# Two decode layers: evacuations on ACT alone, another order of the last weight tiles, and a parked weight copied back by one engine

## The chip, the cores and the metric

One core of a Trainium2 chip runs the whole program. Time is device microseconds of one execution; lower is better. All data is fp32. PE is the matmul engine, DVE and ACT are the two engines that can read the matmul's accumulators in PSUM, SP issues the DMAs.

## The reference

Batch 8, one new token each, two layers that share their weights. A layer is attention over a cache of 4096 keys (32 query heads, 4 key heads, 128 wide) and then a GELU network of 3584 hidden columns, each with a layernorm ahead and a residual.

```python
x = A_x                                   # [8, 1, 1024]
x = x + _A_ref(_layernorm(x), k_cache, v_cache, wq, wo)   # q = x@wq, softmax(q k) v, @wo
x = x + _B_ref(_layernorm(x), w1, b1, w2, b2)             # gelu(x@w1 + b1) @ w2 + b2
x = x + _A_ref(_layernorm(x), k_cache, v_cache, wq, wo)
x = x + _B_ref(_layernorm(x), w1, b1, w2, b2)
```

## The kernel before

All that is read from memory goes through one list of transfers (`stream`), written out by hand with a fixed place for each in one large SBUF tile, `arena` (52 units of 128 x 1024). `pump` issues the transfers in that order on SP's queue: the next one goes out as soon as its place is free, and what is behind it in the list waits. A place becomes free where the program calls `release`, behind the last matmul that reads it. So PE's order decides when SP may issue.

Since only 8 rows of x are there, matmuls use 32 of the array's columns, and four of them work side by side on four column groups, which write the four 32-row quarters of one PSUM bank. An fp32 matmul stands in the trace as two rows.

- `expand` (L256): h = x @ w1 in seven groups `u` of 512 hidden columns. A group's eight matmuls (L263) read one w1 tile of 2 MB; the accumulator is scaled into a row, half by DVE (L273) and half by ACT (L274); `hidden_group` transposes it (L284), sums its quarters (L330), and computes bias and GELU on DVE and ACT up to h (L336), eight columns of `hT` for each of 28 tiles `kt`. `work` is a table of what stands between the matmuls of a group and behind its evacuation. In layer 1 the last w1 tile comes in two halves.
- `down` and `down_row`: h @ w2. w2 lies in four blocks `c` of 256 output columns. Most of it is read once, in layer 0, and stays for layer 1; the first four tiles of each block (kind `"u"`, 512 KB each) are read again for layer 1 and are the last four transfers of the program. `down_row` (L389) multiplies tiles of h with all four blocks, block `c` in column group `c`. `grow_u` does this for the pieces, one block after the other.
- `swap` is between the layers. It finishes the w2 blocks of layer 0 one by one (L383), copies each (L426), turns it with PE (L430) and adds it to x (L432); as soon as two tiles `kt` of x are there, it multiplies them with wq for layer 1 (`used`, L299), tile by tile and for two accumulators `u`, and so frees the places in which wq lay since the start. `late` holds one such step until behind the next block's copy. The places are taken by w2's own blocks 1 to 3 and, behind them, by the first tiles of k of layer 1.
- The last wq tile doesn't fit in the arena: `park` keeps a part of it in PSUM (`spot`, 128 x 2048) and a part in the SBUF tile `spare`. `unpark` (L647, L648) copies `spot` back to the arena, into the place of wq tile (3,1).

Of the kernel before, what the change touches and what calls it, by code (L numbers as in the profile page):

```python
# [9 lines left out]
AF = mybir.ActivationFunctionType  # L10
ALU = mybir.AluOpType
# [4 lines left out]
B, D = 8, 1024  # L16
# [4 lines left out]
NFT = F // P  # L21
CH = 512
HALF = SK // 2
NH = SK // HALF
W = HALF // P * DH
# [16 lines left out]
CB = D // Q4  # L42
# [3 lines left out]
NGR = F // G  # L46
GT = G // P
# [57 lines left out]
def decode_layers(ctx: ExitStack, tc: tile.TileContext, x, kc, vc, wq, wo, w1, w2, out):  # L105


    nc = tc.nc
# [38 lines left out]
    hT = oT  # L147
# [107 lines left out]
    def expand(name, rs, lag, work={}):  # L255
        rows = [row_s, qz[:, 2 * GT * B:2 * GT * B + CH]]  # L256
        for u in range(NGR):
            acc = ps_o.tile([P, CH], F32, tag="o", name="acc")
            kt = 0
            for i, slot in enumerate(tiles((name, u))):  # L260
                for c in range(0, slot.cols, G):
                    j = kt % 4
                    nc.tensor.matmul(acc[32 * j:32 * j + 32, :], xnT[:, kt * XS:kt * XS + 32], slot.ap[:, c:c + G],  # L263
                                     start=(kt < 4), stop=(kt >= NT - 4))
                    kt += 1
                release(slot)
                for f in work.get((u, i), ()):
                    f()
            assert kt == NT
            row = rows[u % 2]  # L270
            if u == 0:
                flush()
            nc.vector.tensor_scalar(row[:, 0:CH // 2], acc[:, 0:CH // 2], rs, None, op0=ALU.mult)  # L273
            nc.scalar.activation(row[:, CH // 2:], acc[:, CH // 2:], AF.Copy, scale=rs)  # L274
            if lag:
                flush()
            pending.append(lambda u=u, row=row: hidden_group(u, row))
            for f in work.get(u, ()):
                f()
# [25 lines left out]
    def queries(rs):  # L305
# [16 lines left out]
            into_qz(u, lambda e, dst: nc.vector.tensor_copy(dst, src[:, e * REP:(e + 1) * REP, 0:B]))  # L322
        rows.free()

    def hidden_group(u, row):
        src = turned(row).rearrange("p (t j) q -> p t q j", j=4)[:, :, 0:B]
        t0 = u * GT
        pre, g = qz[:, 0:GT * B], qz[:, GT * B:2 * GT * B]
        pre_v = pre.rearrange("p (t b) -> p t b", b=B)
        nc.vector.tensor_reduce(pre_v, src, AX.X, ALU.add)  # L330
        nc.vector.tensor_tensor(pre_v, pre_v, b1T[:, t0:t0 + GT].unsqueeze(2).to_broadcast([P, GT, B]), ALU.add)
        nc.vector.tensor_tensor(g, pre, pre, ALU.mult)
        nc.vector.scalar_tensor_tensor(g, g, 1.0 / GELU_A, pre, op0=ALU.add, op1=ALU.mult)
        nc.scalar.activation(g, g, AF.Tanh, scale=GELU_C * GELU_A)
        nc.vector.tensor_scalar(pre, pre, 0.5, None, op0=ALU.mult)
        nc.vector.scalar_tensor_tensor(hT[:, t0 * B:(t0 + GT) * B], g, 1.0, pre, op0=ALU.add, op1=ALU.mult)  # L336
        if u == NGR - 1 and st["layer"] == 0:
            nc.gpsimd.memset(qz[:, 0:2 * GT * B + CH], 0.0)

# [37 lines left out]
    w2_at = {}  # L377

    def down(y, c, kts, n0=0):

        for n, kt in enumerate(kts, n0):
            g = kt % 4
            nc.tensor.matmul(y[32 * g:32 * g + 32], hT[:, kt * B:kt * B + 32], w2_at[c, kt], start=(n < 4), stop=(n >= NFT - 4))  # L383

    def down_row(y, kts, cs=range(CB)):

        for kt in kts:
            for c in cs:
                nc.tensor.matmul(y[32 * c:32 * c + 32], hT[:, kt * B:kt * B + 32], w2_at[c, kt],  # L389
                                 start=st["y0"][c], stop=(kt == NFT - 1))  # L390
                st["y0"][c] = False

    def arrive(c, kind):
        kts = W2_KTS[kind]
# [5 lines left out]
    def swap():  # L400

        ys = small_ps("s")
        down(ys[:, 0:Q4], 0, arrive(0, "u"), 0)
        flush()
        nc.vector.tensor_tensor(xv, xv, b2T.unsqueeze(2).to_broadcast([P, NT, B]), ALU.add)
        pt = small_ps("pt")
        late = []
        acc = q_acc()
        stats = ()

        def used(kt, u):
            slot = held.pop(("q", kt, u))
            q_part(acc, u, kt, 0, slot.ap)
            release(slot)
            if (kt, u) == (3, 1):
                st["unparked"] = unpark()

        for c in range(CB):
            y = ys[:, c % 2 * Q4:(c % 2 + 1) * Q4]
            kts = []  # L420
            for kind in W2_ORDER[c]:
                kts += arrive(c, kind) if c or kind != "u" else []
            down(y, c, kts, NFT - len(kts))
            release(held.pop(("w2u0", c)))
            ysb = row_s[:, c % 2 * Q4:(c % 2 + 1) * Q4]
            nc.vector.tensor_copy(ysb, y)  # L426
            while late:
                late.pop()()
            for i in range(2):
                nc.tensor.matmul(pt[:, i * B:(i + 1) * B], ysb[:, i * P:(i + 1) * P], bsel, start=True, stop=True)  # L430
            xc = xv[:, 2 * c:2 * c + 2]
            nc.vector.tensor_tensor(xc, pt[:, 0:2 * B].rearrange("p (i b) -> p i b", b=B), xc, ALU.add)  # L432
            if c == CB - 1:
                stats = moments(pt)
            for kt in (2 * c, 2 * c + 1):
                for u in range(2):
                    if kt < NT - 1:
                        late.append(lambda kt=kt, u=u: used(kt, u))
                        if c == CB - 1 or (kt, u) not in ((1, 1), (3, 1)):
                            late.pop()()  # L440
                    elif u == 0:
                        spot = st.pop("unparked")
                        q_part(acc, u, kt, 0, spot.ap)
                        spot.free()
                    else:
                        slot = held.pop(("qe", 0))
                        q_part(acc, u, kt, 0, slot.ap[:, 0:W - KEEP])
                        q_part(acc, u, kt, W - KEEP, spare)
                        slot.free()
                    if c == CB - 1 and (kt, u) in ((NT - 2, 1), (NT - 1, 0)):  # L450
                        next(stats, None)
        arena.own_at = OWN[1]
        dl, rs, tmp = (oT[:, a:a + n] for a, n in ((192, B), (200, B), (0, REP * B)))
        rows = arena.own()
        row = [rows.ap[:, u * CH:(u + 1) * CH] for u in range(2)]
        nc.vector.tensor_copy(row[0], acc[0])
        nc.scalar.activation(row[1], acc[1], AF.Copy)
        for u in range(2):
            src = turned(row[u], ("s", "pt")[u])

            def emit(e, dst):
                t = src[:, e * REP:(e + 1) * REP]
                v = tmp.rearrange("p (t b) -> p t b", b=B)
                nc.vector.tensor_tensor(v, t[:, :, B:XS].to_broadcast([P, REP, B]), dl.unsqueeze(1).to_broadcast([P, REP, B]), ALU.mult)
                nc.vector.tensor_tensor(v, t[:, :, 0:B], v, ALU.subtract)
                nc.vector.tensor_tensor(dst, v, rs.unsqueeze(1).to_broadcast([P, REP, B]), ALU.mult)

            into_qz(u, emit)
        rows.free()
# [174 lines left out]
    def unpark():  # L644
        spot = st.pop("spot")
        slot = arena.take(2, OWN[1][0:1])
        nc.scalar.activation(slot.ap[:, 0:W // 2], spot[:, 0:W // 2], AF.Copy)  # L647
        nc.vector.tensor_copy(slot.ap[:, W // 2:], spot[:, W // 2:])  # L648
        return slot

    def weights(name, dram, sizes, starts, c0=0, i0=0, kept=None):
# [85 lines left out]
    for layer in range(2):  # L737
# [9 lines left out]
        if layer == 0:  # L747
            expand("i0", rs, True)
            swap()
        else:  # L750
            nc.vector.tensor_tensor(x_row, x_row, b2_row, ALU.add)
            y = []

            def grow(u):
                if not y:
                    y.append(small_ps("s")[:, 0:Q4])
                    st["y0"] = [True] * CB
                down_row(y[0], groups[u])

            def grow_u(*cs):  # L760
                for c in cs:
                    arrive(c, "u")
                    down_row(y[0], groups[0], [c])

            groups = [range(GT * u, GT * (u + 1)) for u in range(NGR)]
            work = {0: [flush], 1: [flush], **{u: [lambda u=u: grow(u - 1), flush] for u in range(2, NGR - 1)},
                    (NGR - 1, 0): [lambda: grow(NGR - 2)], NGR - 1: [flush, lambda: grow_u(*range(CB))]}
            expand("i1", rs, False, work)
            down_row(y[0], groups[NGR - 1])
            nc.vector.tensor_tensor(x_row, x_row, y[0], ALU.add)  # L770

    nc.sync.dma_start(out=out, in_=x_row)
# [68 lines left out]
```

## Time and profile before

| | |
|---|---|
| median of 3 runs | 859.35 us (859.25 to 860.32) |
| the profiled execution | 858.83 us, its span 856.9 us |
| PE, DVE, ACT busy | 539.4, 198.8, 63.4 us |
| DMA | 359.55 MB, mean 420 GB/s |
| granted PE clock, mean | 0.801 |

The span is the stretch from the first to the last instruction on the profiled core; the execution's own time is 1.9 us longer. Times in rows of the trace are counted from the span's start. A row of the timeline has start, duration, engine, line, operation, out<-in, shape and count, and in brackets how long the engine had been idle and who ended that. Rows that follow each other and overlap are merged with their count.

### The profile page before, as it was taken

Reading aid. Unit: us, or ns where it says so; the run is one execution under the profiler, and the core shown is the slowest. Engines: PE = TensorE matmul, PEld = TensorE weight load, DVE = VectorE, ACT = ScalarE, POOL = GpSimd, SP = SyncE. Lnnn points to the kernel's source line nnn. Section 1 sums busy time; section 2 is a strip of 40 time slices with the busy share of each in tenths; the row PEclk is TensorE's granted clock in tenths of the full one; section 3 lists DMA queues with packets and bytes.
Section 4 is the critical chain, followed back from the end, with each engine's and each line's share of the span. In section 5 each row is a group of like instructions: output and inputs, shape, how many; then the busy total and the mean of one; then the engine's idle time right before and its main releaser. Section 6 shows DMA issues by size and latency. Waiting matters only on the chain.

```text
span 856.9 us, 9313 instructions
## 1 busy us (share of the span) xinstructions
PE 539.4 (63%) x4002; PEld 185.5 (22%) x4002; DVE 198.8 (23%) x689; ACT 63.4 (7%) x136; POOL 2.2 (0%) x13
## 2 busy tenths in 40 slices
PE   0766665576665656755778786556565484664687
PEld 0212121121212111222233233112111121121333
DVE  0012232222222122300320342223212132231032
ACT  0110000000000000001101100000000000000020
POOL 0000000000000000000000000000000000000000
PEclk9976877867876768788888987769778687787889
DMA  9999999999999999999999999999999999999994
GB/s 398 420 437 435 419 436 428 426 431 427 428 429 433 434 431 426 424 428 426 423 397 360 423 434 423 450 418 431 432 426 426 431 428 448 420 425 433 421 424 194
DMA packets 19768, 359.55 MB, mean 420 GB/s; under 512 B 2192, under 2 KB 2576, under 8 KB 3600
## 3 DMA queue, kind: packets, MB, share of 16 engines
q1 hardware_dynamic: 19584, 358.82, 98.4%
q8 instruction: 31, 0.51, 0.2%
q10 hardware_dynamic: 144, 0.15, 0.1%
q14 instruction: 9, 0.07, 0.0%
HBM read 358.83 MB, written 0.13 MB: 419 GB/s over the span
## 4 chain that ended last, share of the span: by engine, by line
DMA 72%; PE 23%; DVE 2%; issue 1%; ACT 1%; another core or an unknown queue 1%; SPq 0%; ACTq 0%; DVEq 0%
DMA arena<-in_k_dram 27%; DMA arena<-in_v_dram 22%; DMA arena<-in_wo_dram 10%; DMA arena<-in_w_dram 9%; PE sps L509 8%; PE o_ps L565 7%; DMA arena<-in_wq_dram 5%; PE acc L299 2%; PE y L346 2%; PE sps L389 1%; PE sps L541 1%; PE acc L263 1%; PE sps L383 1%; ACT arena L532 1%
## 5 line engine op out<-in xcount | busy, mean ns | idle before, releaser
L565 PE MATMUL o_ps<-arena 128*32 128x512 f32 x1024 | 165.8, 772 | 83.0 <-DMA arena<-in_v_dram 82.9
L509 PE MATMUL sps<-arena,qz 128*32 128x512 f32 x1024 | 149.3, 724 | 95.2 <-DMA arena<-in_k_dram 93.8
L509 PEld LDWEIGHTS sps<-arena,qz 128*32 128x32 f32 x1024 | 32.7, 125 | 177.2 <-DMA arena<-in_k_dram 100.5
L570 DVE SCALAR_TENSOR_TENSOR scr<-o_ps,bits,scr 128x128 f32<-128x128 f32 x192 | 67.4, 351 | 6.8
L565 PEld LDWEIGHTS o_ps<-arena 128*32 128x32 f32 x1024 | 33.7, 131 | 147.9 <-issue 115.1
L568 DVE TENSOR_SCALAR scr<-o_ps,bits 128x128 f32<-128x128 f32 x64 | 22.5, 351 | 171.4 <-PE o_ps L565 171.4
L532 ACT ACTIVATE arena<-arena,bits 128x512 f32<-128x512 f32 x32 | 22.8, 714 | 525.0 <-DVE scr L527 525.0
L346 PE MATMUL y<-arena,oxT 128*32 128x256 f32 x512 | 40.7, 478 | 32.6 <-DMA arena<-in_wo_dram 32.6
L514 DVE TENSOR_SCALAR_CACHE_REDUCE arena<-sps 128x512 f32<-128x512 f32 x32 | 22.1, 692 | 147.8 <-PE sps L509 147.8
L541 PE MATMUL sps<-ident,arena 128*128 128x128 f32 x128 | 28.9, 382 | 24.6 <-ACT arena L532 24.3
L263 PE MATMUL acc<-arena,oxT 128*32 128x512 f32 x224 | 34.6, 743 | 14.2 <-DMA arena<-in_w_dram 13.7
L299 PE MATMUL acc<-arena,oxT 128*32 128x512 f32 (+1 forms) x250 | 35.7, 707 | 6.6 <-DMA arena<-in_wq_dram 3.5
L577 PEld LDWEIGHTS sps<-bits,scr 128*128 128x128 f32 x128 | 20.7, 203 | 66.6 <-issue 36.9
L346 PEld LDWEIGHTS y<-arena,oxT 128*32 128x32 f32 x512 | 18.6, 133 | 52.4 <-DMA arena<-in_wo_dram 36.1
L578 DVE TENSOR_TENSOR oxT<-sps,scr 128x8 f32<-128x8 f32 x64 | 10.6, 165 | 72.5 <-PE sps L577 72.5
L541 PEld LDWEIGHTS sps<-ident,arena 128*128 128x128 f32 x128 | 20.3, 190 | 30.3 <-ACT arena L532 30.2
L577 PE MATMUL sps<-bits,scr 128*128 128x8 f32 x128 | 26.5, 280 | 0.0
L523 PE MATMUL sps<-scr,bits 128*128 128x128 f32 x32 | 8.3, 344 | 22.8 <-DVE scr L519 22.8
L545 DVE COPY arena<-sps 128x512 f32<-128x512 f32 x16 | 11.1, 692 | 29.7 <-PE sps L541 29.7
L383 PE MATMUL sps<-arena,oxT 128*32 128x256 f32 x224 | 14.8, 398 | 4.4 <-DMA arena<-in_w_dram 4.4
L199 PE MATMUL sps<-ident,xb 128*128 128x128 f32 x6 | 1.5, 345 | 24.6 <-DMA xb<-in_x_dram 23.5
L389 PE MATMUL sps<-arena,oxT 128*32 128x256 f32 x224 | 15.9, 380 | 0.6 <-DVE oxT L336 0.6
(115 smaller groups left out, 221.0 us busy)
## 6 DMA issues: line engine op xcount, KB each, us to landing
arena<-in_v_dram SPq DMA_DIRECT2D x19, 4096.0 KB, 18.6
arena<-in_k_dram SPq DMA_DIRECT2D x31, 2048.0 KB, 17.3
arena<-in_k_dram SPq DMA_DIRECT2D x12, 4096.0 KB, 17.5
arena<-in_w_dram SPq DMA_DIRECT2D x17, 2048.0 KB, 12.6
arena<-in_v_dram SPq DMA_DIRECT2D x4, 6144.0 KB, 25.4
arena<-in_v_dram SPq DMA_DIRECT2D x11, 2048.0 KB, 20.6
arena<-in_wo_dram SPq DMA_DIRECT2D x10, 2048.0 KB, 12.6
arena<-in_k_dram SPq DMA_DIRECT2D x2, 6144.0 KB, 23.6
```

What stands on the lines that cost most here:

```text
L263: nc.tensor.matmul(acc[32 * j:32 * j + 32, :], xnT[:, kt * XS:kt * XS + 32], slot.ap[:, c:c + G], start=(kt < 4), stop=(kt >= NT - 4))
L299: nc.tensor.matmul(acc[u][32 * j:32 * j + 32, d0 - j * CH:d1 - j * CH], xnT[:, kt * XS:kt * XS + 32], ap[:, d0 - c0:d1 - c0], start=(kt == ...
L346: nc.tensor.matmul(y[32 * j:32 * j + 32, 0:Q4], lhs[:, n * B:n * B + 32], slot.ap[:, c + j * Q4:c + (j + 1) * Q4], start=(n == 0), stop=(n ...
L383: nc.tensor.matmul(y[32 * g:32 * g + 32], hT[:, kt * B:kt * B + 32], w2_at[c, kt], start=(n < 4), stop=(n >= NFT - 4))
L389: nc.tensor.matmul(y[32 * c:32 * c + 32], hT[:, kt * B:kt * B + 32], w2_at[c, kt], start=st["y0"][c], stop=(kt == NFT - 1))
L509: nc.tensor.matmul(ps[32 * g:32 * g + 32, :], qz[:, c:c + 32], kt[:, g * CH:(g + 1) * CH], start=(j == 0), stop=(j == HKV - 1))
L532: nc.scalar.activation(part, part, AF.Exp, bias=bias, scale=1.0, accum_out=ls[:, h:h + 1])
L541: nc.tensor.transpose(pp[:, t * P:(t + 1) * P], row[:, c:c + P], ident)
L565: nc.tensor.matmul(o[32 * g:32 * g + 32, :], s[:, g], v[:, g * CH:(g + 1) * CH], start=(half == 0), stop=(half == NH - 1))
L568: nc.vector.tensor_scalar(r, o[:, 0:P], sel_t[:, 0:1], None, op0=ALU.mult)
L570: nc.vector.scalar_tensor_tensor(r, o[:, t * P:(t + 1) * P], sel_t[:, t:t + 1], r, op0=ALU.mult, op1=ALU.add)
L577: nc.tensor.matmul(po[:, 0:REP], r_s[j % 2], sel_h, start=True, stop=True)
```

## The change

- In `expand` ACT alone scales all 512 columns of a group into the row; DVE's half is gone (14 instructions on DVE in both layers, and the one in `unpark`).
- In layer 1's end both halves of the last w1 tile are multiplied at once. The w2 products of group 5 follow in two halves, one ahead of and one behind the transposes of the last group; then those of group 6; and the four late pieces (group 0) at the very end, tile by tile over the four blocks.
- h of the last group goes to columns of `spare` in layer 1.
- In `swap`, wq (1,1) is no longer held back, `spot` is copied back by ACT alone, and that step is called behind wq (4,0) in place of (3,1).

```diff
-            nc.vector.tensor_scalar(row[:, 0:CH // 2], acc[:, 0:CH // 2], rs, None, op0=ALU.mult)
-            nc.scalar.activation(row[:, CH // 2:], acc[:, CH // 2:], AF.Copy, scale=rs)
+            nc.scalar.activation(row, acc, AF.Copy, scale=rs)
...
+    def h_at(kt):
+        if st["layer"] and kt >= NFT - GT:
+            return spare[:, 2 * CH + (kt - NFT + GT) * B:]
+        return hT[:, kt * B:]
...
-    def down_row(y, kts, cs=range(CB)):
+    def down_row(y, kts):
         for kt in kts:
-            for c in cs:
-                nc.tensor.matmul(y[32 * c:32 * c + 32], hT[:, kt * B:kt * B + 32], w2_at[c, kt],
-                                 start=st["y0"][c], stop=(kt == NFT - 1))
-                st["y0"][c] = False
+            for c in range(CB):
+                nc.tensor.matmul(y[32 * c:32 * c + 32], h_at(kt)[:, 0:32], w2_at[c, kt],
+                                 start=(kt == GT), stop=(kt == GT - 1))
...
-            if (kt, u) == (3, 1):
+            if (kt, u) == (4, 0):
                 st["unparked"] = unpark()
...
-                        if c == CB - 1 or (kt, u) not in ((1, 1), (3, 1)):
+                        if (kt, u) != (3, 1):
                             late.pop()()
...
-        nc.scalar.activation(slot.ap[:, 0:W // 2], spot[:, 0:W // 2], AF.Copy)
-        nc.vector.tensor_copy(slot.ap[:, W // 2:], spot[:, W // 2:])
+        nc.scalar.activation(slot.ap, spot, AF.Copy)
...
-            def grow_u(*cs):
-                for c in cs:
-                    arrive(c, "u")
-                    down_row(y[0], groups[0], [c])
+            end = groups[NGR - 2]
             work = {0: [flush], 1: [flush], **{u: [lambda u=u: grow(u - 1), flush] for u in range(2, NGR - 1)},
-                    (NGR - 1, 0): [lambda: grow(NGR - 2)], NGR - 1: [flush, lambda: grow_u(*range(CB))]}
+                    NGR - 1: [lambda: down_row(y[0], end[:2]), flush, lambda: down_row(y[0], end[2:])]}
             expand("i1", rs, False, work)
             down_row(y[0], groups[NGR - 1])
+            for c in range(CB):
+                arrive(c, "u")
+            down_row(y[0], groups[0])
```

PE's order in `swap`, from the first block's w2 to the third block's turn, before (x12 at L299 are three wq steps of four matmuls, x28 at L383 a block of w2, x2 at L430 the turn):

```order
L383 MATMUL sps<-arena,oxT 32x256 x24
L430 MATMUL sps<-bits,scr 128x8 x2
L299 MATMUL acc<-arena,oxT 32x512 x12
L383 MATMUL sps<-arena,oxT 32x256 x28
L299 MATMUL acc<-arena,oxT 32x512 x4
L430 MATMUL sps<-bits,scr 128x8 x2
L299 MATMUL acc<-arena,oxT 32x512 x12
```

The same place after:

```order
L388 MATMUL sps<-arena,oxT 32x256 x24
L434 MATMUL sps<-bits,scr 128x8 x2
L298 MATMUL acc<-arena,oxT 32x512 x16
L388 MATMUL sps<-arena,oxT 32x256 x28
L434 MATMUL sps<-bits,scr 128x8 x2
L298 MATMUL acc<-arena,oxT 32x512 x12
```

wq (1,1), four matmuls, has moved from behind block 1's w2 to ahead of it.

PE's order at the end of the program, before (L263 is w1, L284 the transposes, L389 w2; scr and qz are the two rows that take turns):

```order
L284 MATMUL sps<-ident,qz 128x128 x4
L263 MATMUL acc<-arena,oxT 32x512 x4
L389 MATMUL sps<-arena,oxT 32x256 x16
L263 MATMUL acc<-arena,oxT 32x512 x4
L284 MATMUL sps<-ident,scr 128x128 x4
L389 MATMUL sps<-arena,oxT 32x256 x32
```

The same place after:

```order
L283 MATMUL sps<-ident,qz 128x128 x4
L263 MATMUL acc<-arena,oxT 32x512 x8
L394 MATMUL sps<-arena,oxT 32x256 x8
L283 MATMUL sps<-ident,scr 128x128 x4
L394 MATMUL sps<-arena,oxT 32x256 x8
L394 MATMUL sps<-arena,spare 32x256 x16
L394 MATMUL sps<-arena,oxT 32x256 x16
```

The last four matmuls with w1 stand directly behind the first four; group 5's sixteen with w2 are split around the transposes; the late pieces are the last sixteen, where before they were the first sixteen of the last 32. SP's order of transfers is the same in both.

More of the change, by code (lines that the diff above doesn't have):

```diff
@@ L335, in hidden_group @@
         nc.vector.tensor_scalar(pre, pre, 0.5, None, op0=ALU.mult)
-        nc.vector.scalar_tensor_tensor(hT[:, t0 * B:(t0 + GT) * B], g, 1.0, pre, op0=ALU.add, op1=ALU.mult)
+        nc.vector.scalar_tensor_tensor(h_at(t0)[:, 0:GT * B], g, 1.0, pre, op0=ALU.add, op1=ALU.mult)
         if u == NGR - 1 and st["layer"] == 0:
@@ L382, in down @@
             g = kt % 4
-            nc.tensor.matmul(y[32 * g:32 * g + 32], hT[:, kt * B:kt * B + 32], w2_at[c, kt], start=(n < 4), stop=(n >= NFT - 4))
-    def down_row(y, kts, cs=range(CB)):
+            nc.tensor.matmul(y[32 * g:32 * g + 32], h_at(kt)[:, 0:32], w2_at[c, kt], start=(n < 4), stop=(n >= NFT - 4))
+    def down_row(y, kts):
         for kt in kts:
-            for c in cs:
-                nc.tensor.matmul(y[32 * c:32 * c + 32], hT[:, kt * B:kt * B + 32], w2_at[c, kt],
-                                 start=st["y0"][c], stop=(kt == NFT - 1))
-                st["y0"][c] = False
+            for c in range(CB):
+                nc.tensor.matmul(y[32 * c:32 * c + 32], h_at(kt)[:, 0:32], w2_at[c, kt],
+                                 start=(kt == GT), stop=(kt == GT - 1))
     def arrive(c, kind):
@@ L756, in grow @@
                     y.append(small_ps("s")[:, 0:Q4])
-                    st["y0"] = [True] * CB
                 down_row(y[0], groups[u])
-            def grow_u(*cs):
-                for c in cs:
-                    arrive(c, "u")
-                    down_row(y[0], groups[0], [c])
             groups = [range(GT * u, GT * (u + 1)) for u in range(NGR)]
+            end = groups[NGR - 2]
             work = {0: [flush], 1: [flush], **{u: [lambda u=u: grow(u - 1), flush] for u in range(2, NGR - 1)},
-                    (NGR - 1, 0): [lambda: grow(NGR - 2)], NGR - 1: [flush, lambda: grow_u(*range(CB))]}
+                    NGR - 1: [lambda: down_row(y[0], end[:2]), flush, lambda: down_row(y[0], end[2:])]}
             expand("i1", rs, False, work)
             down_row(y[0], groups[NGR - 1])
+            for c in range(CB):
+                arrive(c, "u")
+            down_row(y[0], groups[0])
             nc.vector.tensor_tensor(x_row, x_row, y[0], ALU.add)
```

## The prediction

> **What bounds the kernel now.** I read the page's queue and chain parts first.
>
> ```profile
> q1 hardware_dynamic: 19584, 358.82, 98.4%
> DMA 72%; PE 23%; DVE 2%; issue 1%; ACT 1%; another core or an unknown queue 1%; SPq 0%; ACTq 0%; DVEq 0%
> ```
>
> The transfers take 98.4% of 16 engines' span: the kernel is one stream of 358.82 MB, and only two things can move its time: stretches in which the stream stands still, and what follows its last byte. I looked for both in the table by stage.
>
> ```profile
> core 0: us, PE busy (x) PEld busy (x) DVE busy (x) ACT busy (x) POOL busy (x), PEclk, DMA share, GB/s
> 465.30:467.60 2.30, 2.30 (x16) 0.64 (x12) 0.00 (x0) 0.00 (x0) 0.00 (x0) 0.50 0.36 101
> 844.00:846.00 2.00, 1.94 (x29) 0.65 (x20) 0.00 (x0) 0.00 (x0) 0.00 (x0) 1.00 0.55 217
> 846.00:848.00 2.00, 1.32 (x7) 0.70 (x8) 0.85 (x3) 0.47 (x1) 0.00 (x0) 1.00 0.21 86
> 848.00:850.00 2.00, 2.00 (x19) 1.17 (x18) 0.87 (x5) 0.23 (x1) 0.00 (x0) 1.00 0.00 0
> ```
>
> There is one hole in mid-kernel (share 0.36 around 466 us), in `swap`, and a tail: the stream thins from 844 us on and is over at 848, 8.9 us ahead of the end of the span. In the tail some of the 16 engines are done (share 0.55, then 0.21) while others still move the last pieces, so a landing is that of the slowest engine. When do the last pieces land? The issue line by itself, for the second half of the last w1 tile and for the last w2 piece:
>
> ```profile
> L236 SPq DMA_DIRECT2D arena<-in_w_dram x1: 328/328/328, 816.5 to 816.5; - x1
> DMA to landing us min/median/max: 25.8/25.8/25.8
> ...
> L236 SPq DMA_DIRECT2D arena<-in_w_dram x1: 328/328/328, 827.6 to 827.6; - x1
> DMA to landing us min/median/max: 20.5/20.5/20.5
> ```
>
> So the last w1 half is there at 816.5 + 25.8 = 842.3 us and the last piece at 827.6 + 20.5 = 848.1. The timeline of the tail shows what PE, DVE and ACT do with them:
>
> ```profile
> 840.92 0.66 PE L284 MATMUL sps<-ident,qz 128*128 128x128 f32 x4
> 841.51 1.06 PE L263 MATMUL acc<-arena,oxT 128*32 128x512 f32 x8
> 841.61 0.29 DVE L330 TENSOR_REDUCE qz<-sps 128x32 f32<-128x128 f32 x1 [1.80 <-PE sps L284]
> 843.15 1.93 PE L389 MATMUL sps<-arena,oxT 128*32 128x256 f32 x32 [0.58 <-DVE oxT L336]
> 844.90 1.04 PE L263 MATMUL acc<-arena,oxT 128*32 128x512 f32 x8
> 846.01 0.48 DVE L273 TENSOR_SCALAR scr<-acc,bits 128x256 f32<-128x256 f32 x1 [2.92 <-PE acc L263]
> 846.55 1.01 PE L284 MATMUL sps<-ident,scr 128*128 128x128 f32 x4 [0.61 <-DVE scr L273]
> 846.59 0.47 ACT L274 ACTIVATE scr<-acc,bits 128x256 f32<-128x256 f32 x1 [3.75 <-DVE scr L273]
> 847.49 6.32 PE L389 MATMUL sps<-arena,oxT 128*32 128x256 f32 x64
> 853.85 0.42 DVE L770 TENSOR_TENSOR xb<-xb,sps 128x256 f32<-128x256 f32 x1 [4.77 <-PE sps L389]
> ```
>
> An fp32 matmul stands as two rows, so a w2 group of 16 is x32. PE runs the first half of the last w1 tile at 841.51, waits for h of group 5 (ready 843.15), multiplies it with w2, and only then takes the second half, which has lain there since 842.3. The last 64 rows (the late pieces, then group 6) take 6.32 us. The same two groups at 843.15's pace, 1.75 from start to the next start (844.90 - 843.15) and 1.93 for the second, would take 3.68.
>
> **The change part by part.** *The late pieces over four column groups.* Before, the loop goes piece by piece: all its matmuls of one column block write the same 32 rows of PSUM. After, the column block is the inner loop, as in every other group here. The term is 6.32 - 3.68 = 2.64 us, all on the path, since nothing stands between the last matmul (853.81) and the sum at 853.85.
>
> *Last w1 tile first.* After: first half 841.51, second half right behind it (landed 842.3) at 842.38 by 1.75/2 for 8 rows, done for the next matmul at 843.25. Half of group 5's w2 follows (h ready 843.15): to 844.12. ACT alone turns the accumulator from about 843.5:
>
> ```profile
> L319 ACT ACTIVATE arena<-acc,bits 128x512 f32<-128x512 f32 x1 | 0.7, 687 | 0.3 <-PE acc L299 0.3
> ```
>
> The same form (128x512, scaled by a column) takes 0.69, done at 844.2. Four transposes go until about 844.8 (0.59 from start to the next start, 840.92 to 841.51 in group 5), the other half of group 5 to 845.65. From the reduction to h ready is 841.61 to 843.15 for group 5, 1.54; here the reduction starts at 844.9 (0.10 behind 844.8, as 841.61 is behind 841.51), so h of group 6 is ready at 846.45. Group 6 runs there instead of from 847.49 on: 1.04 earlier. Its 1.75 ends at 848.20, just behind the last landing at 848.1: the pieces are hidden by 0.1 only, and what is late next is their transfer; behind a wait for it on PE only the pieces themselves are queued, and DVE's sum. The last matmul ends at 848.20 + 1.93 = 850.1 against 853.81. Tail: -3.7; I book -3.6, as landing and PE are so close. The own buffer for h alone costs and brings nothing: without it the write at 846.2 would wait for group 5's readers, which are through at 845.9.
>
> *ACT alone for the evacuations.* DVE's 0.48 and ACT's 0.47 run in series (846.01 to 847.06: ACT waits for DVE); alone ACT needs 0.69. In the last group this is inside the 1.04 above, about 0.2 of it. The Trainium skill's page TensorEngine Tiling (Array Packing), section PSUM Bottleneck, says to use both ScalarE and VectorE for PSUM evacuation; by that rule two halves side by side would be done after 0.48, ACT alone would lose 0.2, and the sum would be smaller by that. The trace disagrees here: both read one PSUM bank one behind the other. Elsewhere the evacuations lie under the stream; layer 0's chain shows it:
>
> ```profile
> 400.03 11.03 DMA arena<-in_w_dram
> 411.20 1.96 PE acc L263 x16
> 413.18 12.57 DMA arena<-in_w_dram
> ...
> 442.92 5.36 DMA arena<-in_w_dram
> ...
> 449.88 7.25 DMA arena<-in_w_dram
> ```
>
> A slot is released, and SP issues, behind the matmuls (413.18), not behind the evacuation. Twelve or thirteen of the fourteen are worth 0. The rows give the pace as well: landings at 411.06 and 425.75, three 2 MB tiles apart: 4.90 each, 2.45 for 1 MB.
>
> *`swap`: the parked wq copied back by ACT, the copy later, wq(1,1) not held back.* The timeline of the third column block and who holds SP:
>
> ```profile
> 461.16 0.61 PE L430 MATMUL sps<-bits,scr 128*128 128x8 f32 x4
> 461.26 1.02 ACT L647 ACTIVATE arena<-spot 128x1024 f32<-128x1024 f32 x1 [23.66 <-PE acc L299]
> 462.32 1.23 DVE L648 COPY arena<-spot 128x1024 f32<-128x1024 f32 x1 [2.28 <-ACT arena L647]
> 463.46 0.17 DVE L432 TENSOR_TENSOR oxT<-sps,oxT 128x16 f32<-128x16 f32 x1
> 463.68 5.34 PE L299 MATMUL acc<-arena,oxT 128*32 128x512 f32 x32 [1.91 <-DVE oxT L432]
> ...
> SPq L236 <- PE acc L299: 24.1, 7, 7.2
> ...
> L236 SPq DMA_DIRECT2D arena<-in_k_dram x1: 328/328/328, 466.5 to 466.5; - x1
> DMA to landing us min/median/max: 7.3/7.3/7.3
> ...
> L236 SPq DMA_DIRECT2D arena<-in_w_dram x1: 328/328/328, 453.5 to 453.5; - x1
> DMA to landing us min/median/max: 14.4/14.4/14.4
> ```
>
> DVE's half of the copy waits for ACT's, and L432, which PE needs for wq tile 4, is queued behind it on DVE: PE stands 1.91 us. SP can issue the first k tile of layer 1 only when wq(4,1) is used, at 466.5; the stream's last w2 tile lands at 453.5 + 14.4 = 467.9, and the hole is this late issue. The k tile lands at 473.8, 5.9 behind it, where 4.90 + 0.15 for the 64 KB of wq between were needed: 0.85 lost on the slowest engine; the mean of 16 stood 2.30 x (1 - 0.36) = 1.47. After, L432 comes at 461.8, PE 1.7 earlier, and the issue as much earlier at least. ACT's copy of 2048 columns is 1.9 long (1024 take 1.02; the parking copy of 1920 on ACT I scale from that), begun behind wq(4,0), for an operand needed only for tile 7, over 10 us later: free.
>
> wq(1,1) used at once releases its slot some 4 us before 449.88, where the second w2 tile of block 2 is issued. That tile lands at 457.13. The one before it:
>
> ```profile
> L236 SPq DMA_DIRECT2D arena<-in_w_dram x1: 328/328/328, 444.7 to 444.7; - x1
> ...
> DMA to landing us min/median/max: 8.6/8.6/8.6
> ```
>
> It lands at 453.3, so 3.85 pass where 1 MB needs 2.45: 1.4 lost, if the late issue is the cause; 0 if not. Its 8 matmuls (0.9) move ahead of block 1's w2, of which the last piece lands late enough (442.92 + 5.36 = 448.3) to cover them; without that cover they cost 0.9. So the stream gains between -0.9 and, for an engine that stood through the whole hole, 2.3 + 1.4 = 3.7; I take 2.0, close under what the two landings lost (0.85 + 1.4 = 2.25). What comes earlier here comes earlier at every later landing, as nothing else stalls the stream up to the tail.
>
> Sum: -3.6 - 2.0 = -5.6. The profiled execution (858.83, span 856.9 and 1.9 around it) would become 853.2; the median of the runs shown is 0.5 above it, 859.35, and becomes 853.8.
>
> **The rivals.** *The stream gives the gain of `swap` back*: each landing is that of the slowest of 16 engines, and the hole may only let that one catch up; for it speaks that the tail's share falls from 0.55 to 0.21 before the last landing. Then the tail alone: 859.35 - 3.6 = 855.8. *The serial order of the pieces isn't what made them slow*, so the change doesn't do what it says: 1.0 and `swap`'s 2.0 stay, 856.3; without `swap` 858.3, no change. Against it: the 64 rows ran at a granted clock of 1.00, without waits. *Slower*: PE's clock. At 465.30 it was 0.50, and the 32 rows of 512 columns begun at 463.68 took 5.34, where at 1.00 four times eight rows of 1.04 take 4.2 at most. If the waits in the new tail (0.8 for h of group 6) drop it from 844 on to half, the 64 rows take 7.4, what precedes them 2 more, so PE ends at 855.8, 2.0 late: 861.4 if `swap` brings nothing. It decides where PE idles long enough; before it idled 0.6 twice since 843 (the rows of 843.15 and 846.55) and kept 1.00. By the Trainium skill's TensorE: Matmul & The Clock Gate (What's actually happening), the clock falls after an idle window of about 3.4 us; no wait of the new tail is near that, and by that rule this rival is out.
>
> **How the numbers follow.** A difference under 0.2% (1.7 us) can't be told from none here. Forecast (both gains) 0.70, tail alone 0.18, pieces not the cause but `swap` gains 0.05, neither 0.04 (no change), clock 0.03 (slower). Faster is 0.70 + 0.18 + 0.05 = 0.93. The range reaches from the fullest case, 859.35 - 3.7 - 3.7 = 851.9, to the case at 856.3, rounded up to 856.5; left out are 0.07 and the ends of the cases.
>
> **What would show it.** Right: the last 32 + 32 w2 rows in about 3.7 us, PE on the second half of the last w1 tile straight behind the first, evacuations of 0.69 on ACT, L432's successor no longer behind a copy, the first k tile issued before 465, no stage in `swap` with a share near 0.36, the last w2 landing near 846 us. Wrong: w2 rows in the tail still one column block after the other in time, a last landing at 848 or later, a PE clock under 1.00 behind 840 us, or a new wait of SP in `swap`.

## The result, and the profile after

| | before | after |
|---|---|---|
| median | 859.47 us (859.07 to 860.32, 9 runs) | 853.64 us (852.70 to 858.32, 9 runs) |
| ratio | | 0.9941 (0.9924 to 0.9957) |
| the profiled execution | 858.83, span 856.9 | 855.96, span 854.1 |

The change is faster by 5.8 us in the medians, 3.7 to 6.5 by the ratio's interval; 853.8 was forecast. The profiled execution of after isn't a typical one: it is 2.3 us above its median, and the reason is the most instructive part of this case.

First the hole in `swap` and the end of the stream, in the same stretches of the table by stage as before:

```profile
465.30:467.60 2.30, 1.82 (x36) 0.68 (x24) 0.00 (x0) 0.00 (x0) 0.00 (x0) 1.00 0.94 373
844.00:846.00 2.00, 2.00 (x32) 1.09 (x32) 0.20 (x1) 0.69 (x1) 0.00 (x0) 1.00 0.07 27
846.00:848.00 2.00, 1.43 (x28) 0.61 (x24) 1.03 (x6) 0.23 (x1) 0.00 (x0) 1.00 0.00 0
```

The columns are those of the table by stage in the prediction. The DMA share around 466 us is 0.94 in place of 0.36: the hole is gone. The stream is over at 846. The issue lines for the second half of the last w1 tile and for the last w2 piece:

```profile
L236 SPq DMA_DIRECT2D arena<-in_w_dram x1: 327/327/327, 815.2 to 815.2; - x1
DMA to landing us min/median/max: 25.6/25.6/25.6
...
L236 SPq DMA_DIRECT2D arena<-in_w_dram x1: 327/327/327, 826.1 to 826.1; - x1
DMA to landing us min/median/max: 19.7/19.7/19.7
```

Landed at 840.8 and 845.8 (before 842.3 and 848.1). The tail, from the timeline:

```profile
842.31 1.93 PE L263 MATMUL acc<-arena,oxT 128*32 128x512 f32 x16
844.05 1.05 PE L394 MATMUL sps<-arena,oxT 128*32 128x256 f32 x16
844.36 0.69 ACT L273 ACTIVATE scr<-acc,bits 128x512 f32<-128x512 f32 x1 [0.71 <-PE acc L263]
845.10 0.66 PE L283 MATMUL sps<-ident,scr 128*128 128x128 f32 x4
845.69 1.07 PE L394 MATMUL sps<-arena,oxT 128*32 128x256 f32 x16
845.80 0.29 DVE L335 TENSOR_REDUCE qz<-sps 128x32 f32<-128x128 f32 x1 [1.90 <-PE sps L283]
847.33 1.93 PE L394 MATMUL sps<-arena,spare 128*32 128x256 f32 x32 [0.57 <-DVE spare L341]
849.08 1.91 PE L394 MATMUL sps<-arena,oxT 128*32 128x256 f32 x32
851.06 0.42 DVE L771 TENSOR_TENSOR xb<-xb,sps 128x256 f32<-128x256 f32 x1 [3.78 <-PE sps L394]
```

Every step is there as drawn: both halves of the last w1 tile at once, ACT's 0.69, the last 64 rows in 3.66. But they begin at 842.31, 1.5 us behind the landing of the tile's second half, and nothing in the tail waits for a DMA. From that start to PE's end it takes 8.7 us, where before took 12.3 from 841.51: 3.6 saved, and 0.8 of it lost to the late start. The stream's earlier end of 2.3 us buys nothing in this execution.

The last transfer that PE waits for is an earlier one, the w1 tile of group 5. PE's row for it, before and after:

```profile
837.34 1.93 PE L263 MATMUL acc<-arena,oxT 128*32 128x512 f32 x16 [0.65 <-DMA arena<-in_w_dram]
```

```profile
838.14 1.93 PE L263 MATMUL acc<-arena,oxT 128*32 128x512 f32 x16
```

Before, PE waits for the tile (landed at 837.3) and starts at once. After, the tile lands 1.5 us earlier, at 835.8, and PE takes it 2.3 us later than that, without a wait: it was behind with its own work. In those stages the granted clock was low, which the same table shows from layer 1's second layernorm on:

```profile
808.00:812.00 4.00, 1.27 (x16) 0.86 (x20) 1.13 (x6) 1.79 (x3) 0.00 (x0) 0.69 1.02 434
812.00:816.00 4.00, 3.16 (x24) 0.90 (x16) 0.16 (x1) 0.73 (x2) 0.00 (x0) 0.50 0.99 418
816.00:820.00 4.00, 2.34 (x12) 1.12 (x16) 1.05 (x5) 1.72 (x4) 0.00 (x0) 0.50 1.03 434
820.00:824.00 4.00, 3.17 (x16) 0.91 (x8) 0.19 (x1) 0.79 (x2) 0.00 (x0) 0.50 0.99 422
824.00:828.00 4.00, 4.00 (x38) 1.23 (x40) 1.24 (x6) 0.81 (x2) 0.00 (x0) 0.68 1.03 438
```

It was granted 0.50 until after 824, over the first w1 groups. The mean over 808 to 828 is 0.57 here and 0.83 in the profile of before.

### The profile page after: what moved, and what is told of

The parts are those of the page before. It is cut to its first block, busy times and chain, and to the rows that moved or that the text cites. A ratio compares the mean times of both kernels' runs of the same rounds, so it can differ in the third digit from the quotient of the medians.

```text
span 854.1 us, 9301 instructions
## 1 busy us (share of the span) xinstructions
PE 536.7 (63%) x4002; PEld 184.1 (22%) x4002; DVE 190.8 (22%) x674; ACT 67.1 (8%) x136; POOL 2.2 (0%) x13
## 4 chain that ended last, share of the span: by engine, by line
DMA 69%; PE 25%; DVE 2%; ACT 1%; issue 1%; another core or an unknown queue 1%; SPq 0%; ACTq 0%; DVEq 0%
DMA arena<-in_k_dram 27%; DMA arena<-in_v_dram 22%; DMA arena<-in_w_dram 8%; DMA arena<-in_wo_dram 8%; PE sps L513 8%; PE o_ps L569 7%; DMA arena<-in_wq_dram 5%; PE acc L263 2%; PE y L351 2%; PE sps L394 1%; PE sps L545 1%; PE sps L283 1%; PE acc L298 1%; ACT arena L536 1%
## 5 line engine op out<-in xcount | busy, mean ns | idle before, releaser
L263 PE MATMUL acc<-arena,oxT 128*32 128x512 f32 x224 | 36.1, 774 | 13.5 <-DMA arena<-in_w_dram 13.1
L298 PE MATMUL acc<-arena,oxT 128*32 128x512 f32 (+1 forms) x250 | 32.4, 653 | 6.3 <-DMA arena<-in_wq_dram 4.8
L388 PE MATMUL sps<-arena,oxT 128*32 128x256 f32 x224 | 13.7, 381 | 3.1 <-DMA arena<-in_w_dram 3.1
## 6 DMA issues: line engine op xcount, KB each, us to landing
arena<-in_w_dram SPq DMA_DIRECT2D x17, 2048.0 KB, 12.3
```

The lines of the kernel that those rows point to most:

```text
L298: nc.tensor.matmul(acc[u][32 * j:32 * j + 32, d0 - j * CH:d1 - j * CH], xnT[:, kt * XS:kt * XS + 32], ap[:, d0 - c0:d1 - c0], start=(kt == ...
L388: nc.tensor.matmul(y[32 * g:32 * g + 32], h_at(kt)[:, 0:32], w2_at[c, kt], start=(n < 4), stop=(n >= NFT - 4))
```

## The experiments

Each ratio is against the kernel before on the same chip, with its 95% interval.

**The end's edits alone.** The kernel before with `down_row`, `h_at` and the table `work` of after; evacuations and `swap` as before.

> Before with the end's edits alone (order of the last weight tiles, late pieces over four column groups, own buffer for the last h); evacuations by DVE and ACT, swap as before. Theory (two gains that add up, tail 3.6 and swap 2.0): 859.4 - 3.4 (the 0.2 of the evacuation is missing) = 856.0, w2's last 64 rows in 3.7 us, last landing near 848 as before. Rival (the tail hangs on how far PE is behind in the w1 groups, which the clock granted there decides): between 856 and 858.8, different by execution, with the last h and not the last landing as what the late pieces wait for.

Measured: 855.88, ratio 0.9965 (0.9948 to 0.9982), 1.5 to 4.5 us faster. The profiled execution was one with the clock low (0.57 from 808 to 828): the last w1 tile's matmuls begin at 842.37, 7.6 us pass behind the last landing (846.7). The gain is there, as the theory has it, and the time of one execution hangs on PE's start, as the rival has it. The late pieces waited for nothing: they follow group 6 directly.

**The late pieces' loop alone.** Before with

```diff
                 for c in cs:
                     arrive(c, "u")
-                    down_row(y[0], groups[0], [c])
+                down_row(y[0], groups[0])
```

> Before, with the late pieces' loop turned alone: tile by tile over the four blocks in place of block by block; order of the groups as before. Theory: the last 64 rows take 3.7 in place of 6.3 us, minus a wait for the last piece, which is now needed in the first tile (848.1 against 847.5 in the run of before): 859.4 - 2.0 = 857.4. Rival (the pieces were slow for another reason than their column group): 859.4, the rows still 6 us.

Measured: 856.03, ratio 0.9967 (0.9955 to 0.9978). The timeline's row for the last 64:

```profile
848.85 3.66 PE L389 MATMUL sps<-arena,oxT 128*32 128x256 f32 x64
```

3.66 in place of 6.32, with no other edit: the order of the loop was the cause. Two things change with it, the column group and the tile of h from one matmul to the next. `down`, whose 28 matmuls rotate over the four column groups and take another tile of h each time, tells them apart:

```profile
468.84 3.20 PE L383 MATMUL sps<-arena,oxT 128*32 128x256 f32 x56
```

This row of before, at a clock of 1.00, has 0.114 us for a matmul, as the 32 in 3.66 have; so what made the pieces slow is that four matmuls in a row went to one column group. The wait for the last piece that I had subtracted didn't come, since in this execution PE was behind (last w1 tile from 842.88); the median is 1.4 us under what I expected. This one line is worth as much in the median as all of the end's edits together; what the order of groups adds is too small for these runs to tell. In the traces it is there: from the last w1 tile's first matmul to PE's end 12.3 before, 9.6 with this loop, 8.8 with all of the end's edits, 8.7 after.

**`swap`'s edits alone.** Before with `if (kt, u) == (4, 0)` and `if (kt, u) != (3, 1)`, and ACT's copy of all of `spot`.

> Before with swap's three edits alone (ACT copies all of spot, behind wq (4,0), wq (1,1) not held back). Theory: the stream gains, each landing behind 480 us is 2.0 earlier (1 to 3), and so the end: 857.4; first k tile of layer 1 issued at 462 in place of 466.5. Rival (only the engines that were ahead gain, the slowest keeps its time): 859.0 to 859.4 with last landings near 848.

Measured: 857.27, ratio 0.9978 (0.9966 to 0.9989), 0.9 to 2.9 us. The hole is closed. What it had cost is seen within each execution, from the landing of the last w2 tile ahead of the hole to that of the second k tile of layer 1. The issue lines of these two, first with `swap`'s edits, then in a kernel with the old `swap` (the last experiment below):

```profile
L236 SPq DMA_DIRECT2D arena<-in_w_dram x1: 328/328/328, 453.1 to 453.1; - x1
DMA to landing us min/median/max: 15.6/15.6/15.6
...
L236 SPq DMA_DIRECT2D arena<-in_k_dram x1: 328/328/328, 464.5 to 464.5; - x1
DMA to landing us min/median/max: 14.1/14.1/14.1
```

```profile
L236 SPq DMA_DIRECT2D arena<-in_w_dram x1: 328/328/328, 453.2 to 453.2; - x1
DMA to landing us min/median/max: 14.2/14.2/14.2
...
L236 SPq DMA_DIRECT2D arena<-in_k_dram x1: 328/328/328, 466.4 to 466.4; - x1
DMA to landing us min/median/max: 11.6/11.6/11.6
```

By themselves the k tiles land at 478.6 and 478.0, so the one issued earlier is there no earlier. But the stream of the first was already later at the w2 tile, 468.7 against 467.4: between the two landings pass 9.9 us with the edits and 10.6 without. The prediction's pace asks for 9.95 (twice 4.90, and 0.15 for wq). Over all traces it is 9.9 to 10.2 in seven of the eight where ACT alone copies back (the first of after has 10.9), and 10.6 to 11.3 in five of the six with the old copy (before has 12.3). So the old copy costs the stream 0.6 to 1.4 us there, its slowest DMA engine included. The first k tile doesn't show it: it lands 5.0 to 5.1 behind the w2 tile in all but before (5.9) and the first of after (5.4). Up to the landing of group 5's w1 tile the mean is 368.5 us with the old copy and 367.9 with ACT's, with overlapping ranges; the last landing itself scatters more, from 845.4 to 848.1 without ACT's copy and from 845.3 to 846.9 with it.

**Two of `swap`'s edits apart.** Before with the copy back by ACT behind wq (4,0), and before with wq (1,1) used at once.

> Before with the parked weight copied back by ACT alone behind wq (4,0); wq (1,1) still held back. Theory: this carries most of what the three edits in swap bring (1.9 us measured): 857.8, first k tile issued at 464.5. Rival (the early release of wq (1,1)'s place carries it): 859.1.

> Before with wq (1,1) used at once, the copy back as before. Theory: the second w2 tile of block 2 is issued at 445.7 in place of 449.9, but the trace of the kernel with swap's edits lost as much one tile earlier, so that late issue wasn't the cause: 859.0, no difference. Rival (it was): 858.0, with 2.5 us between that tile's landing and the one before it in place of 3.9.

Measured: 857.85, ratio 0.9988 (0.9974 to 1.0003), and 858.87, ratio 1.0007 (0.9996 to 1.0019). wq (1,1) alone brings nothing; the copy's share isn't told from zero in the medians, but its trace has the hole closed (10.0 us between the two landings above, 11.3 with wq (1,1) alone). The tile whose late issue I had charged with 1.4 us, and the one before it, with wq (1,1) still held back and then with it used at once:

```profile
L236 SPq DMA_DIRECT2D arena<-in_w_dram x1: 328/328/328, 444.7 to 444.7; - x1
DMA to landing us min/median/max: 9.7/9.7/9.7
...
L236 SPq DMA_DIRECT2D arena<-in_w_dram x1: 328/328/328, 449.5 to 449.5; - x1
DMA to landing us min/median/max: 7.4/7.4/7.4
```

```profile
L236 SPq DMA_DIRECT2D arena<-in_w_dram x1: 328/328/328, 444.6 to 444.6; - x1
DMA to landing us min/median/max: 9.4/9.4/9.4
...
L236 SPq DMA_DIRECT2D arena<-in_w_dram x1: 328/328/328, 445.5 to 445.5; - x1
DMA to landing us min/median/max: 11.1/11.1/11.1
```

2.5 us between the landings (454.4, 456.9) with the late issue, 2.6 (454.0, 456.6) with the early one: full pace either way. Four more traces with wq (1,1) held back have 2.5 to 3.0. The 3.85 in the trace of before was that execution's own.

**ACT alone.** Before with the one line of `expand`.

> Before with ACT alone for the 14 evacuations of h. Theory: 0.2 earlier at the end, else hidden: 859.2, no difference that can be told. Rival (two engines side by side are faster): 0.2 later, 859.6. Both within the measurement; what tells is the trace: ACT's 0.69 against DVE's 0.48 and ACT's 0.47 in a row.

Measured: 859.21, ratio 1.0008 (0.9994 to 1.0021). The other way round, after with DVE and ACT in halves:

> After with the evacuations by DVE and ACT in halves again. Theory: 0.2 later at most, in the last group alone: 853.8, no difference that can be told. Rival (ACT alone costs in the first w1 groups of layer 1, where its operand comes late): 0.5 earlier.

Measured: 854.42, ratio 0.9938 (0.9923 to 0.9952), the change itself beside it 0.9931 (0.9915 to 0.9948). Both comparisons say the same: no difference that can be told in medians. The traces show 0.09 us at the end (the table below).

**PE's head start and its clock.** After with the first group's transposes behind the second w1 tile, then with four extra matmuls as well, then with those four alone.

```diff
-            work = {0: [flush], 1: [flush], ...
+            work = {1: [flush], ...
```

> After, with one entry of layer 1's table taken out: the first h group's transposes stand behind the second w1 tile's matmuls and no longer ahead of them, so PE doesn't wait there for the layernorm's last steps and the evacuation (2.5 us at 815 in the profile of after). Theory (after's end hangs on how far PE is behind when the clock was granted at 0.50 from 810 to 827 us, and only PE's head start can mend it): 852.7, about 1 us under the change's 853.6, and less scatter; the last w1 tile's matmuls start at about 840.8 in place of 842.3 and the late pieces wait for their landing. Rival (the last landing sets the end anyway): 853.6, no difference.

```diff
+    def heat(n):
+        for _ in range(n):
+            nc.tensor.matmul(st["junk"][:, 0:CH], ident, spare[:, 0:CH], start=True, stop=True)
...
+            if st["layer"] and HQ - 6 <= n < HQ:
+                heat(1)
...
         rs = layernorm(x_row, rsum)
+        if layer:
+            heat(2)
```

> The same, and four matmuls of 512 columns into the dead PSUM tile of the parked weight, in PE's waits ahead of and behind layer 1's second layernorm (0.86 us each at full clock), as load for the clock gate alone. Theory: the granted clock stays 1.00 from 800 us on, the w1 groups wait for their tiles as in the profile of before, 852.4. Rival (the extra matmuls only stand in the way): 853 to 854, clock 0.50 behind 810 us as in after. What would refute the clock as cause: clock at 1.00 and no gain over the reordered kernel and over the change.

> After with the four extra matmuls alone (load for the clock gate), the transposes where the change has them. Theory: clock at 1.00 over more of 800 to 830 us than in the two traces with 17 us at 0.50, 5.5 to 6.5 us behind the last landing, 853.6. Rival: the extra matmuls don't hold the clock, 7.5 or more behind the landing, 854.5.

And the change itself once more:

> The change itself once more, for a second trace and on the chip of the runs beside it. Theory (what the span has behind the last landing hangs on the clock granted from 800 to 830 us): the profiled execution again shows 7.5 to 8.5 us behind the last landing if the clock was at 0.50 for most of that stretch, and 5.5 to 6.5 if it was at 1.00; 853 to 855 in the median. Rival (the 8.3 us of the first trace are the change's own): 8 or more with the clock at 1.00 as well.

Measured: 854.71 (0.9953, 0.9939 to 0.9968), 853.65 (0.9945, 0.9930 to 0.9959), 853.59 (0.9929, 0.9912 to 0.9946), and the change 853.89 (0.9931, 0.9915 to 0.9948). None of them beats the change by what can be measured: 852.7 and 852.4, which the theory had for the first two, were missed, and no gain over the change is one of the two signs that I had named against the clock as the cause. The change once more ended 7.1 us behind its last landing at a clock of 0.56, where 7.5 to 8.5 was expected; the table below shows that the last landing is the wrong place to count from. Their traces show the clock's part in a single execution, though. The stage of the four extra matmuls alone:

```profile
808.00:812.00 4.00, 3.34 (x24) 1.65 (x28) 1.23 (x6) 1.79 (x3) 0.00 (x0) 1.00 1.02 434
812.00:816.00 4.00, 1.48 (x22) 0.69 (x15) 0.16 (x1) 2.32 (x4) 0.00 (x0) 1.00 1.02 426
816.00:820.00 4.00, 3.42 (x20) 0.72 (x18) 1.24 (x6) 0.73 (x2) 0.00 (x0) 0.63 0.98 418
820.00:824.00 4.00, 3.77 (x20) 1.45 (x24) 1.24 (x6) 0.41 (x2) 0.00 (x0) 0.52 1.01 430
824.00:828.00 4.00, 4.00 (x56) 1.67 (x48) 1.05 (x5) 0.87 (x2) 0.00 (x0) 1.00 1.00 426
```

and its tail:

```profile
839.86 1.92 PE L263 MATMUL acc<-arena,oxT 128*32 128x512 f32 x16
844.88 1.93 PE L396 MATMUL sps<-arena,spare 128*32 128x256 f32 x32 [0.57 <-DVE spare L341]
846.63 1.91 PE L396 MATMUL sps<-arena,oxT 128*32 128x256 f32 x32
```

The last w1 tile starts 2.5 us earlier than in the first trace of after, and the last 64 rows with it (844.88 against 847.33). Over all profiled executions, by clock:

| kernel | mean granted clock, 808 to 828 | group 5's w1 tile landed | last w1 tile from | behind that landing | DVE's last sum behind that start | last landing |
|---|---|---|---|---|---|---|
| after once more | 0.56 | 836.1 | 841.2 | 5.1 | 8.75 | 846.0 |
| after | 0.57 | 835.8 | 842.3 | 6.5 | 8.75 | 845.8 |
| the end's edits alone | 0.57 | 836.7 | 842.4 | 5.7 | 8.84 | 846.7 |
| the late pieces' loop alone | 0.57 | 837.2 | 842.9 | 5.7 | 9.70 | 847.2 |
| ACT alone | 0.66 | 835.7 | 840.3 | 4.6 | 12.25 | 845.7 |
| after, evacuation in halves | 0.69 | 836.6 | 840.8 | 4.2 | 8.84 | 846.6 |
| the copy back alone | 0.70 | 835.3 | 839.5 | 4.2 | 12.34 | 845.3 |
| wq (1,1) alone | 0.75 | 835.2 | 839.4 | 4.2 | 12.34 | 845.4 |
| before | 0.83 | 837.3 | 841.5 | 4.2 | 12.34 | 848.1 |
| `swap`'s edits alone | 0.83 | 836.6 | 840.9 | 4.2 | 12.33 | 846.6 |
| after, transposes moved | 0.83 | 836.9 | 841.1 | 4.2 | 8.75 | 846.9 |
| the same and four matmuls | 0.83 | 835.7 | 839.9 | 4.2 | 8.76 | 846.2 |
| after, four matmuls alone | 0.83 | 835.6 | 839.9 | 4.2 | 8.75 | 845.9 |
| the same four, transposes moved, old `swap` | 0.91 | 835.6 | 839.8 | 4.2 | 8.75 | 845.6 |

(Distances are worked out before the times are rounded.) DVE's last sum, behind which only the output leaves, follows the start of the last w1 tile at a distance that hangs on the kernel alone: 12.34 us with the old end, 9.70 with the loop turned, 8.84 with all of the end's edits, and 0.09 less where ACT evacuates alone. The last landing has no part in it. The start in turn is 4.2 behind the landing of group 5's w1 tile wherever the clock was 0.69 or more, and 0.4 to 2.3 later than that in the five executions at 0.66 or less. The three kernels with extra matmuls, which only load PE, have 0.83 or more and no delay. So a low clock is the likely cause of up to 2.3 us, and the end's edits gain 3.5 whatever the clock. The rival, that a late end is the change's own, falls: the same tail starts without delay at 0.69 to 0.91. That the clock doesn't show in the medians of the extra matmuls means that many executions of the change have the high clock anyway, or that the matmuls cost what they bring; the runs don't part these.

**`swap` once more, with the extra matmuls.**

> The kernel with the extra matmuls and the moved transposes, but swap as before. There the end follows the last landing closely, so this tells whether swap's edits make the stream end earlier. Theory: they do by about 1.9 (the median gained by swap's edits alone), 855.6 against 853.7. Rival (they don't: last landings in the traces were 845.7 to 848.1 without and 845.8 to 846.9 with the edits): 853.7, no difference.

Measured: 855.13, ratio 0.9948 (0.9931 to 0.9965). Beside it in the same runs the change with four extra matmuls has 0.9929 (0.9912 to 0.9946), 1.6 us less by the ratios with overlapping intervals, but with the transposes in the other place; the same kernel with `swap`'s edits had 0.9945 (0.9930 to 0.9959) on another chip. Neither expectation is refuted. The old `swap`'s hole around 466 us is smaller in this trace than in before's; PE's clock was 1.00 there, while in the other five traces with the old copy it falls to 0.50 for a part of 460 to 468. In the eight with ACT's copy it stays at 1.00.

```profile
465.30:467.60 2.30, 2.30 (x40) 1.15 (x36) 0.00 (x0) 0.00 (x0) 0.00 (x0) 1.00 0.95 320
```

## Why the prediction was right, point by point

- *The late pieces* (2.64): right, 6.32 to 3.66 us, and shown alone: 12.34 to 9.70 in the table, 1.9 to 3.9 us in the runs.
- *Last w1 tile first* (1.04): 0.86 in the traces (9.70 to 8.84 from the tile's start to DVE's last sum); not told apart in medians. The sum's end was tied to two things that don't hold it. The start at 841.5 was taken over from before; it is 839.4 to 842.9 in these traces, by the landing of group 5's w1 tile and by how far the clock lets PE fall behind. And the last landing, which the sum left only 0.1 ahead of the late pieces, is 0.4 to 3.3 us ahead of them in the eight traces with the new end, so nothing waits for it.
- *ACT alone* (0.2): 0.09 in the traces (12.34 to 12.25; 8.84 to 8.75), nothing in medians. The page TensorEngine Tiling (Array Packing) of the Trainium skill, section PSUM Bottleneck, wants both engines for an evacuation; here the two ran one behind the other on one bank, 0.48 and 0.47 against ACT's 0.69, and two comparisons show no loss from leaving DVE out.
- *`swap`* (2.0): the size is that of the measured 1.9 (0.9 to 2.9), the working only in part. The 0.85 for the hole is borne out in size, though not where I read it: the second k tile loses 0.6 to 1.4 us with the old copy, and the first one lost 0.85 in the trace of before alone. The 1.4 for wq (1,1) was one execution's scatter and is 0. What the measured gain has beyond the hole's part stays open, so it is partly luck that the whole sum comes within 0.2 us of the measured median. The first rival, that the slowest engine keeps its time, has both the landings within executions and the median of `swap`'s edits alone against it.
- *The clock rival*: its place was wrong, and the reason that ruled it out doesn't hold here. The clock fell in the layernorm and the first w1 groups and not in the tail, and the executions that had it low were up to 2.3 us behind. It fell without a wait of 3.4 us: in after it went to half at 809.5, behind 3.41 us in which PE was busy for 1.81, and PE's longest wait from 803 to there was 1.42. By the Trainium skill's TensorE: Matmul & The Clock Gate (What's actually happening) it returns after one busy window of about 3.4 us; here it stayed at 0.50 from 812 to 824 with PE busy for 3.16, 2.34 and 3.17 of 4 us, so such a window has to be fuller than that.

## What to carry to other kernels

Where a kernel is one stream of transfers, look for the last landing that an engine really waits for. Here it isn't that of the last transfer but that of the w1 tile next to last; the time is that landing, what PE is behind at it, and a fixed rest. Work out the three apart, and look at each in several executions. Matmuls that use a quarter of the columns should rotate over the four column groups in program order: a loop turned the wrong way cost 2.7 us for 16 of them. Landings of two executions can't be compared by their times alone, since the streams have drifted apart by then; compare the distance from a landing ahead of the place in question.

## What the runs showed of the hardware

The half clock doesn't need an idle PE to come, nor a PE without any break to go. These stretches of 3.41 us are from after, ahead of the fall at 809.50 and at half clock around 821, and from before, each directly ahead of a return to 1.00:

```profile
806.09:809.50 3.41, 1.81 (x28) 1.05 (x28) 1.15 (x6) 0.07 (x1) 0.00 (x0) 1.00 1.02 432
819.74:823.15 3.41, 2.61 (x16) 0.22 (x8) 0.42 (x3) 0.92 (x2) 0.00 (x0) 0.50 1.02 432
```

```profile
812.73:816.14 3.41, 3.17 (x16) 0.90 (x20) 0.00 (x0) 0.01 (x1) 0.00 (x0) 0.50 1.02 432
819.56:822.97 3.41, 2.90 (x16) 0.43 (x8) 1.38 (x6) 0.23 (x1) 0.00 (x0) 0.50 1.02 432
```

PE busy for 1.81 of 3.41 us lost the full clock; 2.61 didn't bring it back, 2.90 and 3.17 did. These few rows don't give a limit. Four extra matmuls ahead of that stage kept it at 1.00 until 816. Single executions of the same kernel on one core differ by up to 5.6 us here (852.70 to 858.32). In the profiled ones, PE being behind makes up to 2.3 of such a difference, and the landing that it follows another 2 (835.2 to 837.3).
